# The order of the units in a projection of memory rows, their value stores, and the stack of their staging pools

## The chip, the cores and the metric

One core of one Trainium2 chip. The metric is the device time of one execution of the whole program in microseconds (us), the median of several runs. A profiled execution gives the trace; its times count from the first instruction of the span.

## The reference

Two independent parts are computed and joined along the last axis. Part A is a long convolution (H3), part B a transformer with a recurrent memory, in segments of 32 rows:

```python
def _A_ref(q, k, v, shift_k, ssm_k, ssm_D):          # 2048 x 1024
    ...                                              # k_shift: causal convolution of k with 4 taps
    kv = k_shift * v
    ...                                              # y: causal convolution of kv with ssm_k, by FFT of length 4096
    y = y + kv * ssm_D[None, None, :]
    return q * y

def _B_ref(x, mem0, Wq, Wk, Wv, Wo, seg_len):        # x 2048 x 1024, 32 heads of 128, 8 memory rows, seg_len 32
    ...
    mem = mem0
    for s in range(n_seg):                           # 64 segments
        xs = x[:, s * seg_len:(s + 1) * seg_len, :].copy()
        h = jnp.concatenate([mem, xs], axis=1)       # 40 rows
        q = jnp.einsum('btd,dhe->bhte', h, Wq)
        k = jnp.einsum('btd,dhe->bhte', h, Wk)
        v = jnp.einsum('btd,dhe->bhte', h, Wv)
        ...                                          # masked softmax attention within the 40 rows
        o = jnp.einsum('bhte,hed->btd', o, Wo)
        mem = o[:, :M, :].copy()
        outs.append(o[:, M:, :])
```

Each segment needs the memory rows that the segment before it gives, so the 64 segments run one after the other.

## The kernel before

The program has a prologue, which computes part A and prepares part B, and then the loop over the 64 segments. The order of the instructions on every engine is the order in which the program text issues them.

**What is prepared for part B.** Of a segment's 40 rows the first 32 (8 memory rows and 24 of x) are projected within the segment. The last 8 rows of all segments depend on x alone, so they are projected together in the prologue: hTB holds them transposed, 1024 by 512 (8 rows of each of 64 segments). This is the class `Rows` (L127). Its work is cut into 12 *units* (L85), one for each of queries (q), keys (k) and values (v) and each of four groups g of eight heads. A unit has eight steps j of eight matmuls of 128x512 each, and `half` (L155) does half a step, four matmuls; so there are 192 halves. The matmuls of the q and k units are on L177, those of the v units on L174. PSUM has two tiles for them. After every second half the sum is copied to a staging tile by `evac` (L148), on ACT (L150), or, in the last stage, on ACT and DVE by turns (L152).

The q unit and the k unit of a group write into the same staging tile stq (16 KB a partition), which is taken when a q unit begins (L168). When the k unit ends, one transfer on ACT's queue (L185) stores it to QKBd in DRAM, 2 MB in pieces of 256 bytes. A v unit writes the staging tile stv (8 KB a partition), taken when the unit begins (L170). When it ends, 16 transfers of 64 KB on POOL's queue (L190) store it to VBd. Both pools have one buffer each, so the next q unit's first copy waits for the last store from stq, and the next v unit's for the stores from stv. In the tail, the value staging also serves once as park_s (L671).

**Where the weights come from.** A unit needs eight pieces of 128x1024. `load_to` (L132) issues their loads on SP some pieces ahead. Pieces of *resident* weight pairs stay in SBUF for the whole program; pieces of *streamed* and *parked* pairs go into the small ring pring of eight buffers and are loaded again later. Resident pairs get their place in steps, as part A frees memory: `open_res` (L99) opens 9, 10, 3, 12, 2 and at the end the remaining 9 pairs, early ones first and then in the order in which the units use them (L94, L96). `relay` (L116) copies streamed pairs to a compact DRAM copy, from POOL's queue.

**The prologue's stages and the halves that each takes in between:**
- a0 (from L257): tables, and the first transform of ssm_k; no halves.
- a1 (L484 to L502): shift convolution and first transform of kv; 76 halves: q0, k0, v0, q1 and 12 of k1.
- c2 (L597 to L613): the frequency stage, one half in each of 36 steps: the rest of k1, v1, v2. In each step DVE forms products (L572), POOL or DVE adds them to Yre and Yim (L575, L576), and TensorE transforms back (L585).
- c3 (L617 to L648): the output stage, 8 halves ahead and 40 within 16 steps t: v3, q2, k2. A step loads zt and qt on SP (L629, L631), does halves, then the last transform (L644), a product on DVE (L647) and a store to the output on POOL (L648).
- the tail (L665 to L693): the last 32 halves, q3 and k3, and in between the parked weights, which are transposed (L687, L688, L691) and kept in PSUM.

Then all pools of the prologue are closed (L695), a ring of five 4 KB tiles (wring) is opened for the streamed weights and the last nine resident pairs are opened behind it (L696, L697). Before the first segment SP issues five loads into the ring (L713), the first read of QKBd (L793) and the 18 half loads of the nine Wo pairs (L113), in this order; POOL issues the first read of VBd (L803). Within the segments each ring tile that has been used is loaded anew (L713), so SP's queue carries the weight stream, 17 pairs of 512 KB a segment, of which two come from PSUM instead in turn with it.

**The stack of the staging pools.** SBUF pools grow from both ends. The pools of the projection lie at the right end; opened in the order hTB (8 KB), stq (16 KB), pring (16 KB), stv (8 KB), so stv lies lowest, next to the memory that the ring and the last nine pairs get from the left. The ring's 20 KB and the nine pairs' 36 KB cover 8 KB that c3 used and these 48 KB. With the order before, the ring covers stv and the lowest 4 KB of pring; the nine pairs cover the rest of pring, stq and hTB. The ring waits tile by tile for what it covers (`reuse_waits="tile"`), the pool of the nine pairs as a whole.

Of the kernel before, what the change touches and what calls it, by code (L numbers as in the profile page):

```python
# [21 lines left out]
def fused_kernel(ctx: ExitStack, tc, q, k, v, shift_k, ssm_k, ssm_D, outa, x, mem0, Wq, Wk, Wv, Wo, outb, n_seg):  # L22
# [11 lines left out]
    nc = tc.nc  # L34
# [18 lines left out]
    VBd = dram.tile([n_seg, 4, 4, 8, 256], BF, name="VBd")  # L53
# [9 lines left out]
    def half_src(key, n):  # L63
# [3 lines left out]
        if m == "v":  # L67
# [7 lines left out]
    mask = const.tile([128, 2, 40], BF, name="mask")  # L75
    make_identity(nc, ident[:])
    cp = ExitStack()
    hb = cp.enter_context(tc.tile_pool(name="b_hb", bufs=1, side="right"))
    hTB = hb.tile([128, 8, n_seg * 8], BF, name="hTB")
    stq = cp.enter_context(tc.tile_pool(name="b_stq", bufs=1, side="right"))  # L80
    pring = cp.enter_context(tc.tile_pool(name="b_pring", bufs=8, side="right"))
    stv = cp.enter_context(tc.tile_pool(name="b_stv", bufs=1, side="right"))
    ps_p = cp.enter_context(tc.tile_pool(name="b_ps_p", bufs=2, space=PSUM, side="right"))

    units = [("q", 0), ("k", 0), ("v", 0), ("q", 1), ("k", 1), ("v", 1), ("v", 2), ("v", 3),  # L85
             ("q", 2), ("k", 2), ("q", 3), ("k", 3)]

    def piece(i):
        (m, g), kc = units[i // 8], i % 8
# [37 lines left out]
    class Rows:  # L127
# [27 lines left out]
        def half(self, n, by="A"):  # L155

            for _ in range(n):
                if self.at == 192:
                    return
                iu, j, lo = self.at // 16, self.at % 16 // 2, self.at % 2 * 4  # L160
                m, g = units[iu]
                self.load_to(iu * 8 + 8)
                ws = self.loaded[iu * 8:iu * 8 + 8]
                assert len(ws) == 8
                if lo == 0:
                    self.ps = ps_p.tile([128, 512], F32, tag="pp", name="ps_" + m)
                if m == "q" and self.at % 16 == 0:
                    self.st = stq.tile([128, n_seg, 8, 2, 8], BF, tag="stq", name="stq")  # L168
                if m == "v" and self.at % 16 == 0:
                    self.sv = stv.tile([128, 4, 1024], BF, tag="stv", name="stv")  # L170
                rb, cs = j // 2, slice(j % 2 * 512, j % 2 * 512 + 512)
                for kc in range(lo, lo + 4):
                    if m == "v":
                        nc.tensor.matmul(self.ps[:], lhsT=hTB[:, kc, rb * 128:(rb + 1) * 128], rhs=ws[kc][:, cs],  # L174
                                         start=(kc == 0), stop=(kc == 7))
                    else:
                        nc.tensor.matmul(self.ps[:], lhsT=ws[kc][:, j * 128:(j + 1) * 128], rhs=hTB[:, kc, :],  # L177
                                         start=(kc == 0), stop=(kc == 7))
                if lo:
                    if m == "v":  # L180
                        self.evac(self.sv[:, rb, cs], self.ps[:], by)
                    else:
                        self.evac(self.st[:, :, j, int(m == "k"), :], self.ps[:].rearrange("e (s r) -> e s r", r=8), by)
                    if m == "k" and j == 7:
                        nc.scalar.dma_start(QKBd[:, :, g, :].rearrange("s e x -> e s x"),  # L185
                                            self.st[:].rearrange("e s h t r -> e s (h t r)"))
                    if m == "v" and j == 7:
                        for rb_ in range(4):
                            for c in range(4):
                                nc.gpsimd.dma_start(VBd[16 * rb_:16 * rb_ + 16, c, g],  # L190
                                                    self.sv[:, rb_, c * 256:(c + 1) * 256])
                self.at += 1
                self.load_to(self.at // 16 * 8 + 8 + self.at % 16 // 2 + 4)

# [62 lines left out]
    with ExitStack() as ck:  # L257
# [185 lines left out]
        for t in range(17):  # L443
# [16 lines left out]
            if t in (8, 10, 12, 14):  # L460
                rb = t // 2 - 4
# [535 lines left out]
@with_exitstack  # L997
def kernel(
    ctx: ExitStack,
    tc: tile.TileContext,  # L1000
    A_q: bass.AP,
    A_k: bass.AP,
    A_v: bass.AP,
    A_shift_k: bass.AP,
    A_ssm_k: bass.AP,
    A_ssm_D: bass.AP,
    B_x: bass.AP,
    B_mem0: bass.AP,
    B_Wq: bass.AP,
    B_Wk: bass.AP,  # L1010
    B_Wv: bass.AP,
    B_Wo: bass.AP,
    B_seg_len,
    out: bass.AP,
):
    assert int(B_seg_len) == 32
    S = B_x.shape[1]
    n_seg = S // 32
    outa = out[0, :, 0:1024]
    outb = out[0, :, 1024:2048]  # L1020
    with ExitStack() as fctx:
        fused_kernel(fctx, tc, A_q[0], A_k[0], A_v[0], A_shift_k, A_ssm_k, A_ssm_D, outa, B_x[0], B_mem0[0],
                     B_Wq.rearrange("d h e -> d (h e)"), B_Wk.rearrange("d h e -> d (h e)"),
                     B_Wv.rearrange("d h e -> d (h e)"), B_Wo.rearrange("h e d -> (h e) d"),
                     outb, n_seg)
# [35 lines left out]
```

## Time and profile before

| | us |
|---|---|
| median of 3 runs | 2194.64 |
| lowest and highest run | 2191.91, 2197.0 |
| the profiled execution | 2189.17 |
| its span, first to last instruction | 2187.2 |
| TensorE busy (matmuls) | 1783.4 (82% of the span) |
| VectorE busy | 1090.5 (50%) |
| ScalarE busy | 835.3 (38%) |
| GpSimd busy | 405.9 (19%) |
| moved by DMA | 732.15 MB, mean 335 GB/s |

The page's chain of waits has PE with 47% and DMA with 36% of the span; its dearest line is the stream of value weights into the ring (17%).

Names in the profile: PE is TensorE (PEld its weight loads), DVE VectorE, ACT ScalarE, POOL GpSimd, SP the engine that issues most loads; "q" behind a name is that engine's queue of transfers. `out<-in` names the tile written and the tile read, L with a number the line of the kernel; copies by `evac` all have its lines (L150, L152), so they are told apart by their tiles. The clock is the share of full speed that TensorE was granted. In a list of waits the three numbers are the total, the times and the longest, in us.

### The profile page before, as it was taken

How to read it: one execution, taken by the hardware profiler on the slowest of the kernel's cores; microseconds unless marked ns; L12 is line 12 of the kernel's file. 1: busy time of each engine (PE TensorE's matmuls, PEld its weight loads, DVE VectorE, ACT ScalarE, POOL GpSimd, SP SyncE). 2: the span in 40 equal slices, each digit the busy share in tenths (PEclk: the TensorE clock that was granted, in tenths of full speed). 3: DMA queues.
4: the chain of work that ended last, by engine and by line, in shares of the span. 5: the costliest groups of instructions: out<-in, count | busy, mean ns of one | idle time of the engine just before them, and what ended most of it. 6: DMA issues, size and time to landing. Idle time of an engine off the chain costs nothing.

```text
span 2187.2 us, 87959 instructions
## 1 busy us (share of the span) xinstructions
PE 1783.4 (82%) x37808; PEld 1048.2 (48%) x37808; DVE 1090.5 (50%) x3235; ACT 835.3 (38%) x2538; POOL 405.9 (19%) x841
## 2 busy tenths in 40 slices
PE   5777778758888888888888888888888888888889
PEld 2332223325555555554555555545555555555558
DVE  6885652224454555544455455444554545444540
ACT  5445551123333333333444333333333333334320
POOL 4013562101111111111111111111111111111110
PEclk8989899879999999999999999999999999999999
DMA  7798969889999999999999999999999999999990
GB/s 256 266 312 273 314 233 330 267 288 353 347 356 343 373 374 365 368 364 347 370 372 371 370 354 370 362 358 355 368 366 354 363 356 357 371 362 367 359 335 21
DMA packets 275653, 732.15 MB, mean 335 GB/s; under 512 B 65680, under 2 KB 85024, under 8 KB 275262
## 3 DMA queue, kind: packets, MB, share of 16 engines
q1 hardware_dynamic: 214414, 683.05, 84.7%
q0 software_dynamic: 18368, 28.88, 4.2%
q10 hardware_dynamic: 42480, 14.62, 2.7%
q8 instruction: 295, 4.83, 0.9%
q14 instruction: 96, 0.78, 0.1%
HBM read 676.14 MB, written 59.18 MB: 336 GB/s over the span
## 4 chain that ended last, share of the span: by engine, by line
PE 47%; DMA 36%; issue 6%; DVE 4%; ACT 4%; POOL 1%; SPq 0%; ACTq 0%; DVEq 0%; POOLq 0%
DMA wring<-Wstv 17%; PE qkacc L750 13%; PE yacc L867 9%; DMA wring<-Wstqk 7%; PE vacc L765 4%; PE otacc L850 3%; PE yacc L765 3%; PE tp L779 3%; PE pl L984 3%; DMA QKBd<-stq 2%; DMA H<-in_B_x_dram 2%; PE ps_k L177 2%; PE otacc L852 1%; DMA wring<-Wsto 1%; PE ps_q L177 1%
## 5 line engine op out<-in xcount | busy, mean ns | idle before, releaser
L750 PE MATMUL qkacc<-Wqk,hT 128*32 128x512 bf16 x4096 | 351.8, 384 | 3.6 <-issue 3.5
L855 ACT CAST OT<-otacc 128x80 bf16<-128x80 f32 x1024 | 183.8, 235 | 387.4 <-PE otacc L852 381.3
L858 POOL COPY OL<-OT 128x64 bf16<-128x64 bf16 x252 | 63.9, 253 | 1362.3 <-ACT OT L855 1362.3
L765 PEld LDWEIGHTS <-hT 128*32 128x32 bf16 x8192 | 213.8, 97 | 168.7 <-issue 101.9
L750 PEld LDWEIGHTS <-hT 128*32 128x32 bf16 x8192 | 178.3, 96 | 209.9 <-issue 66.7
L867 PE MATMUL yacc<-Wo,OT 128*32 128x256 bf16 x5632 | 253.3, 282 | 26.6 <-issue 21.2
L867 PEld LDWEIGHTS <-OT 128*32 128x32 bf16 x8192 | 213.1, 99 | 90.4 <-issue 58.4
L750 PE MATMUL qkacc<-wring,hT 128*32 128x512 bf16 x2048 | 207.1, 390 | 22.7 <-DMA wring<-Wstqk 20.3
L850 PE MATMUL otacc<-PT,vsb 32*128 32x64 bf16 x2048 | 147.7, 193 | 55.5 <-ACT OT L855 48.7
L765 PE MATMUL vacc<-wring,hT 128*32 128x256 bf16 x2560 | 118.0, 277 | 74.7 <-DMA wring<-Wstv 73.5
L788 DVE COPY QT<-tp 128x256 bf16<-128x256 bf16 x256 | 74.7, 292 | 204.7 <-PE tp L779 198.7
L719 ACT COPY wring<-park 128x1024 bf16<-128x1024 bf16 x128 | 129.9, 1015 | 116.2 <-PE qkacc L750 110.0
L750 PE MATMUL qkacc<-Wearly,hT 128*32 128x512 bf16 x2048 | 167.7, 403 | 7.7 <-DVE hT L893 3.4
L756 ACT CAST qks<-qkacc 128x512 bf16<-128x512 f32 x256 | 150.3, 587 | 47.6 <-PE qkacc L750 44.5
L823 DVE TENSOR_REDUCE mx<-S 128x4 f32<-128x160 f32 x256 | 83.1, 325 | 163.8 <-PE S L820 160.7
L765 PE MATMUL vacc<-Wv,hT 128*32 128x256 bf16 x3584 | 158.4, 274 | 0.7 <-issue 0.7
L834 DVE TENSOR_REDUCE sm<-P 128x4 f32<-128x256 bf16 x256 | 107.5, 420 | 100.6 <-ACT P L832 100.6
L852 PE MATMUL otacc<-PT,VB 32*128 32x64 bf16 x2048 | 144.2, 189 | 11.2 <-issue 10.5
L867 PE MATMUL yacc<-wring,OT 128*32 128x256 bf16 x2520 | 137.1, 281 | 16.4 <-issue 15.4
L885 DVE COPY hT<-x_tp 128x192 bf16<-128x192 bf16 (+1 forms) x64 | 23.0, 359 | 233.8 <-PE x_tp L884 233.8
L970 POOL DMA_DIRECT2D out_dram<-Y_sb x256 | 129.1, 511 | 39.6 <-ACT Y_sb L964 36.3
L850 PEld LDWEIGHTS <-vsb 32*128 32x128 bf16 x2048 | 84.3, 92 | 103.8 <-issue 94.1
(220 smaller groups left out, 2931.9 us busy)
## 6 DMA issues: line engine op xcount, KB each, us to landing
wring<-Wstqk SPq DMA_DIRECT2D x448, 512.0 KB, 6.4
wring<-Wstv SPq DMA_DIRECT2D x320, 512.0 KB, 6.0
wring<-Wsto SPq DMA_DIRECT2D x315, 512.0 KB, 6.0
SK<-s_sb SPq DMA_DIRECT2D x8, 1024.0 KB, 6.5
SU<-s_sb SPq DMA_DIRECT2D x8, 1024.0 KB, 7.8
QKBd<-stq ACTq DMA_DIRECT2D x4, 2048.0 KB, 16.3
Kg<-SK SPq DMA_DIRECT2D x16, 512.0 KB, 6.1
Ug<-SU SPq DMA_DIRECT2D x16, 512.0 KB, 7.2
```

What stands on the lines that cost most here:

```text
L719: nc.scalar.copy(t[:, 0, :], park[key][0][:])
L750: nc.tensor.matmul(u.qk[p0:p0 + 32, :], lhsT=hT[:, kc, :], rhs=w[t][:, c2 * 512:(c2 + 1) * 512], start=(kc == 0), stop=(kc == 7), tile_pos ...
L756: nc.scalar.copy(u.qks[:], u.qk[:])
L765: nc.tensor.matmul(u.vacc[32 * c:32 * c + 32, 0:256], lhsT=hT[:, kc, :], rhs=w[kc % 2][:, c * 256:(c + 1) * 256], start=(kc == 0 and Y is ...
L788: nc.vector.tensor_copy(u.QT[:].rearrange("e (c j) r -> e c j r", c=2), tv[:, 0])
L823: nc.vector.tensor_reduce(out=mx[:], in_=S[:], op=ALU.max, axis=AX.X)
L834: nc.vector.tensor_reduce(out=sm[:], in_=P[:], op=ALU.add, axis=AX.X)
L850: nc.tensor.matmul(o, lhsT=u.v[r, i * 128:(i + 1) * 128], rhs=PTv[r, i, 0], start=True, stop=False, tile_position=(32 * c, 0))
L852: nc.tensor.matmul(o, lhsT=VB[r, i * 128:(i + 1) * 128], rhs=PTv[r, i, 1], start=False, stop=True, tile_position=(32 * c, 0))
L855: nc.scalar.copy(u.OT[:, 2 * c:2 * c + 2, :], ov[:, :, 0:40])
L867: nc.tensor.matmul(Y[32 * dq:32 * dq + 32, 256:512], lhsT=u.OT[:, hh, 0:32], rhs=w[hh % 2][:, dq * 256:(dq + 1) * 256], start=(u.g == 0 an ...
L970: nc.gpsimd.dma_start(outb[32 * s:32 * s + 24, dq * 256:(dq + 1) * 256], Y_sb[32 * dq + 8:32 * dq + 32, :])
```

## The change

Three edits in the prologue. The units are taken group by group, q, k, v of group 0, then of group 1, and so on; before, v2 and v3 came right behind v1, and q2, k2, q3, k3 last. The 16 stores of a v unit, issued together behind its last copy, become four times four, each behind the copies of 128 rows. And the staging pools are opened as stq, stv, hTB, pring, so that pring lies lowest and stq at the very end.

```diff
     cp = ExitStack()
+    stq = cp.enter_context(tc.tile_pool(name="b_stq", bufs=1, side="right"))
+    stv = cp.enter_context(tc.tile_pool(name="b_stv", bufs=1, side="right"))
     hb = cp.enter_context(tc.tile_pool(name="b_hb", bufs=1, side="right"))
     hTB = hb.tile([128, 8, n_seg * 8], BF, name="hTB")
-    stq = cp.enter_context(tc.tile_pool(name="b_stq", bufs=1, side="right"))
     pring = cp.enter_context(tc.tile_pool(name="b_pring", bufs=8, side="right"))
-    stv = cp.enter_context(tc.tile_pool(name="b_stv", bufs=1, side="right"))
     ps_p = cp.enter_context(tc.tile_pool(name="b_ps_p", bufs=2, space=PSUM, side="right"))
 
-    units = [("q", 0), ("k", 0), ("v", 0), ("q", 1), ("k", 1), ("v", 1), ("v", 2), ("v", 3),
-             ("q", 2), ("k", 2), ("q", 3), ("k", 3)]
+    units = [(m, g) for g in range(4) for m in "qkv"]
...
-                    if m == "v" and j == 7:
-                        for rb_ in range(4):
-                            for c in range(4):
-                                nc.gpsimd.dma_start(VBd[16 * rb_:16 * rb_ + 16, c, g],
-                                                    self.sv[:, rb_, c * 256:(c + 1) * 256])
+                    if m == "v" and j % 2 == 1:
+                        for c in range(4):
+                            nc.gpsimd.dma_start(VBd[16 * rb:16 * rb + 16, c, g],
+                                                self.sv[:, rb, c * 256:(c + 1) * 256])
```

The order of the units also sets the order in which resident pairs are opened: the ten pairs that a1 opens, of which the last three were v2's, now end with three of group 2's query and key pairs, c2's three are the rest of those instead of v3's, and c3's twelve are v2's, group 3's query and key pairs and v3's.

## The prediction

> **What bounds the kernel now.** I read the page for its share of engines, then busy time by stage, then the chain of waits in the prologue, then who waits for whom. The page gives a span of 2187.2 us for the profiled execution, whose own time is 2189.17 us, so 2.0 us lie around the span; the median of the runs is 2194.64 us, 5.5 us above it. Sums are made on the profiled execution and carried over to the median as differences.
>
> By stage (from the span's start; columns as in the first line, then granted clock, share of the DMA engines, GB/s):
>
> ```profile
> core 0: us, PE busy (x) PEld busy (x) DVE busy (x) ACT busy (x) POOL busy (x), PEclk, DMA share, GB/s
> 185.00:313.00 128.00, 106.39 (x548) 32.59 (x549) 91.41 (x153) 82.04 (x152) 78.75 (x87) 0.92 0.83 273
> 313.00:393.00 80.00, 58.03 (x249) 24.64 (x247) 17.91 (x15) 13.87 (x24) 25.49 (x49) 0.91 0.95 333
> 393.00:441.00 48.00, 34.02 (x194) 17.04 (x192) 9.90 (x14) 4.76 (x9) 5.81 (x11) 0.86 0.69 222
> 441.00:471.00 30.00, 7.42 (x142) 3.94 (x146) 4.56 (x14) 5.01 (x8) 0.00 (x0) 0.63 0.93 281
> ...
> 545.00:1000.00 455.00, 387.49 (x9598) 236.04 (x9594) 227.87 (x773) 176.16 (x611) 71.22 (x173) 0.96 0.97 360
> ```
>
> The last row is the segment loop: its DMA engines are 97% busy, its TensorE 85%. What it has to move is fixed, so it ends as much earlier as it starts. The change lies in the rows above: the frequency stage c2 (185 to 313), the output stage c3 (313 to 393, DMA share 0.95), a tail of projection (393 to 441), and a start of the loop in which TensorE works 7.4 of 30 us.
>
> The chain of waits shows what holds these stages (start, length, what):
>
> ```profile
> 196.54 20.36 DMA QKBd<-stq
> ...
> 257.31 6.42 DMA VBd<-stv
> ...
> 316.65 6.05 DMA VBd<-stv
> ...
> 393.11 16.26 DMA QKBd<-stq
> ...
> 441.03 11.15 DMA QKBd<-stq
> ```
>
> These are stores of the two staging tiles, each held once, so the next unit of the same kind waits for them. Who waited (total, times, longest):
>
> ```profile
> ACT stv L150 <- DMA VBd<-stv: 19.6, 2, 12.4
> ...
> ACT stq L150 <- DMA QKBd<-stq: 16.4, 1, 16.4
> ...
> PE park_t L687 <- ACT stq L150: 13.2, 1, 13.2
> ...
> PE z_ps L585 <- POOL Yre L575: 8.8, 2, 7.9
> ```
>
> and the same for SP's queue:
>
> ```profile
> SPq L631 <- DVE ot L647: 28.4, 12, 9.5
> SPq L793 <- DMA QKBd<-stq: 24.2, 1, 24.2
> ...
> SPq L678 <- DMA QKBd<-stq: 12.6, 1, 12.6
> ```
>
> The first three are the staging tiles' reuse (v2 behind v1, v3 behind v2, q3 behind k2). L793 is the first read of QKBd in SP's queue: 18 Wo loads and the loop's weight stream stand behind it, and the first segment waits until 470.5 us for a stream tile.
>
> **The change, part by part.** Units keep their count and size: 192 half units of 0.863 us of TensorE, the same loads. The stages take them in fixed numbers, 76 before c2, 36 in c2, 48 in c3, 32 in the tail. So units 0 to 5 do not move; unit 6 (end of c2) turns from v2 into q2, unit 7 from v3 into k2, 8 and 9 from q2, k2 into v2, q3, and the tail from q3, k3 into k3, v3. Resident weight pairs are opened in fixed numbers too (10, 3, 12); the counts come out equal (three pairs of unit 6 or 7 in c2, twelve in c3), so no load is late that was not.
>
> *c2.* Unit 6 no longer writes the value tile, so the wait on v1's 16 stores goes. Its price: the output matmuls (L585) come every 3.07 us (249.10, 252.18, 255.25); behind the wait they come at 266.31, 271.46, 274.53 where 3.07 us steps give 264.46 for the last. **Gain 10.1 us**, 7.9 of idle and the rest at half clock. q2 writes the query tile, whose store landed at 216.9, 40 us earlier. The value stores of v1 now stand on POOL in fours between the products Yre and Yim: 4 x 0.53 = 2.1 us every four halves (12.3 us), where POOL is busy 3 x 1.15 of every 6.14 us and so idle 2.7. I cost them at nothing; were that cover gone, four groups x 2.1 = 8.4 us.
>
> *c3.* The start, where TensorE stood 10.1 us behind v2's stores, I count as nothing by itself: from 320 us the DMA share is 1.01 to 1.03, and the first SZ load took about 14 us, so it would have met the loads anyway. The stage is counted as DMA work.
> Removed: a hole at 356 to 368 us (shares 0.77, 0.36, 0.88: 4.0 us lost), which came as v3's 16 stores stood on POOL ahead of two output stores, DVE's product waited for those (9.8 us), and SP's L631 for DVE (9.5). Groups of four leave room: **4.0 us**. One MB of value stores fewer (before v2 and v3, after v2): at 333 GB/s **3.1 us**.
> Added: k2's query and key store, 2.1 MB, now in the middle (half 128, during t = 3) instead of at the end. Alone it runs at 220 GB/s (444 to 450 us, share 1.05); between 393 and 409.5 the queues moved 326 GB/s where 395 was usual. Below, it costs its bytes at 395, 5.3 us; above, its whole landing, 16.3. I take what that mixture lost, 16.4 x (395 - 326)/395 = 2.9, on top of the bytes, 8.2, say **8.5 us**. And SP stops during such a store: at all three that have something behind them (113, 196.5, 393 us) it issues four to seven more transfers and then stands 12.4, 10.4 and 12.6 us until the landing. What is queued there is zt and qt of later t and weights, and TensorE and DVE wait for these; the engines stay full on what was issued, and only restarting costs: at 216 to 220 the share was 0.46, **2.2 us** (0 to 5).
> Net +8.5 + 2.2 - 4.0 - 3.1 = **+3.6 us** (bounds -1.8 and +18.5). c3 ends at 393.3 - 10.1 + 3.6 = 386.8.
> The Trainium skill, "DMA: Bandwidth & Descriptors", section "Why small descriptors are slow (HBM only)", puts a fixed 3 cycles on a packet of 8 for 256 bytes. By that the store would take 5.3 x 11/8 = 7.3 us and the sum would gain 1.2 us; the 220 GB/s of this trace say more.
>
> *Tail.* Before: 393.3 to 441.0, 47.7 us. The tile wait goes, because k3 writes the tile that q3 already holds, and k2's store is long past: 13.2 us of TensorE idle, and 2.0 us because the 2.2 us of work behind it took 4.2 at a granted clock of 0.50. **15.2 us.** What is late next: the four parked weights. The first was issued 1.1 us after the stage began and landed some 6 us later; the four halves ahead of it take 3.45, so TensorE waits **3.6 us** (0 to 6) where the store had hidden it. The tail is then 47.7 - 15.2 + 3.6 = 36.1, and the projection ends at 422.9.
> The skill's "TensorE: Matmul & The Clock Gate", section "Part 1: The HAM clock gate (the "warmup" mystery)", lets about 3.4 us of idleness bring the half clock back; by that this new wait would cost some 2 us more. The trace grants 0.78 behind a pause of 4.9 us (369.5).
>
> *Behind the last row.* Before, SP's Wo loads began at 452.7, 11.7 after the projection's end, for k3's store. After, k3's store leaves 16 halves (13.8 us) before the end and needs 11.2 alone, so v3 hides it; were v3 not there it would cost the 11.2 again. Instead the nine late weight pairs lie on both staging tiles and hTB, and wait for v3's last row: 4 issues of 0.53 on POOL and a landing of 1.9 to 7.8, 4.0 to 9.9 in all; I take 7.0. **Gain 4.7.** With the restacked pools the ring's three covered tiles lie on the small weight ring pring alone, not on the value tile; the third of its five loads waits for v3's weights and so goes out at the projection's end and lands 3.4 to 6 us later, where its first use stands 2.7 us behind that end (443.7 for 441.0): up to 3 us that fall into the wait for the stream tile, so nothing.
> Value stores of v0 were already leaving pair by pair (from 118.6 on), since POOL had nothing else there: no price.
>
> **Sum**: 10.1 - 3.6 + 15.2 - 3.6 + 4.7 = **22.8 us** less. Profiled execution 2189.2 to 2166.4; for the median 2194.6 - 22.8 = **2172 us**.
>
> **The rivals.**
> *The store in c3 costs its whole landing* (15 in 100). For: c3 is DMA-bound, so nothing hides it; the one at 196.5 landed after 20.4 and stopped TensorE at 216. Against: the engines stayed full meanwhile. 16.3 for 8.5: 15.0 less, 2179.6. The skill's "DMA: Bandwidth & Descriptors", section "Issuing engines are not separate DMA queues", speaks for it: ACT's store runs on the engines that serve SP. The trace agrees (share 1.13 to 1.24 at 399 to 408).
> *Cheaper than bounded* (10): bytes only, no restart, parked weights in time: 3.2 + 2.2 + 3.6 more, 31.8 less, 2163.
> *c2's gain comes back in c3* because loads that the pause let through are then missing (6): DMA share was 0.83 there, which speaks against. 12.7 less, 2182.
> *POOL as the new stop* (6, slower). v2's four groups stand ahead of the output stores just while k2's store slows every landing; each opens a hole as v3's burst did, 9.5 us by L631. 4 x 9.5 = 38: 15 more than before, 2210. It decides from (22.8 + 4.4)/4 = 6.8 us a group on. For: the hole of before is of this kind. Against: it came with 16 stores in a row.
> *It does nothing* (3): the waits move and add up to the same, about 2194; against it stands that three separate waits go.
>
> **How the numbers follow.** My forecast has 60 in 100, its own range 2165 to 2179. With the cheaper case, and most of the first and third rival, 2161 to 2184 leaves out less than 2 in 10. A measurement of this kernel tells a difference from about 0.2%, 4.4 us. Faster by more: 60 + 15 + 10 + 6 = 0.91; within 0.03; slower 0.06.
>
> **What would show it.** Right: no wait of stv or stq on their stores at 257, 316 and 393; SP standing about 10 us in c3 during k2's store; no hole of 9.5 at L631; Wo loads beginning near 430 and the first segment's stall ending near 448. Wrong: c3 longer than 90 us, output stores waiting for value stores, or a segment loop whose pace is not the one before.

## The result, and the profile after

| | before | after |
|---|---|---|
| median of 4 runs each, us | 2193.27 | 2169.79 |
| lowest and highest | 2183.92, 2197.0 | 2166.93, 2172.11 |
| the profiled execution | 2189.17 | 2169.6 |
| its span | 2187.2 | 2167.7 |

The ratio is 0.9898, 95% interval 0.9868 to 0.9928. Of 2193.27 us that is 22.4 us less (the medians themselves differ by 23.5), where the forecast said 22.8.

Two profiles of equal code differ by some microseconds in a1 (the first inverse transform of c2 came between 188.6 and 195.7 us in all kernels here) and in the loop of 1700 us. So the stages are compared by marks of their own, in each kernel's trace: c2 from the first to the last inverse transform (`z_ps<-Yre`), c3 from there to the last `y_ps`, the tail from there to the first segment's `x_tp`, "behind" from `x_tp` to SP's first Wo load, and the way from `x_tp` to the end of the first segment's stall, which contains "behind". "All" runs from the first inverse transform to the end of that stall, and is the sum of the other columns without "behind".

| us | c2 | c3 | tail | behind | x_tp to stall's end | all |
|---|---|---|---|---|---|---|
| before | 117.0 | 83.2 | 48.1 | 11.6 | 29.4 | 277.7 |
| after | 105.7 | 88.3 | 38.7 | 8.1 | 24.5 | 257.2 |
| difference | -11.3 | +5.1 | -9.4 | -3.5 | -4.9 | -20.5 |
| forecast | -10.1 | +3.6 | -11.6 | -4.7 | -4.7 | -22.8 |

The stages give 20.5 us of the 22.4; the rest is well within the interval, which is 6.6 us wide to either side.

Busy time by stage of the changed kernel, to be laid beside that of before (c2, c3, tail, start of the loop, loop):

```profile
core 0: us, PE busy (x) PEld busy (x) DVE busy (x) ACT busy (x) POOL busy (x), PEclk, DMA share, GB/s
185.00:303.00 118.00, 105.69 (x564) 33.21 (x564) 91.82 (x153) 82.67 (x153) 79.75 (x89) 0.98 0.88 297
303.00:390.00 87.00, 58.52 (x243) 24.03 (x241) 20.29 (x17) 12.89 (x22) 17.40 (x32) 0.86 0.98 338
390.00:425.00 35.00, 32.27 (x227) 16.50 (x231) 8.73 (x13) 5.34 (x9) 11.82 (x23) 0.95 0.80 228
425.00:450.00 25.00, 7.20 (x132) 3.62 (x125) 3.87 (x14) 4.14 (x8) 1.37 (x3) 0.70 0.88 321
525.00:980.00 455.00, 384.01 (x9678) 235.65 (x9670) 230.91 (x782) 176.56 (x619) 71.22 (x172) 0.97 0.98 362
```

c2 does the same TensorE work in 118 instead of 128 us, at a clock of 0.98 instead of 0.92. The tail is 35 us with TensorE busy for 32. c3 alone grew. The loop's row is nearly that of before: 98% of the DMA engines and 362 GB/s, for 97% and 360.

The chain of waits between c2 and the loop (start, length, what):

```profile
193.14 19.81 DMA QKBd<-stq
...
384.52 5.93 DMA park_w<-in_B_Wv_dram
...
421.54 7.53 DMA wring<-Wstqk
...
435.21 5.26 DMA Wo<-in_B_Wo_dram
440.54 5.94 DMA wring<-Wstv
```

Of the five stores in the chain of before one is left, k1's. In place of k2's stands the landing of a parked weight, and in place of k3's the ring, Wo and stream loads. The waits from 180 to 460 us (total, times, longest) of the engines:

```profile
PE y_ps L642 <- DMA zt<-SZ: 25.2, 6, 12.1
...
PE park_t L685 <- DMA park_w<-in_B_Wv_dram: 3.4, 1, 3.4
...
PE z_ps L583 <- POOL Yre L573: 0.9, 1, 0.9
```

and of SP's queue:

```profile
SPq L627 <- DMA QKBd<-stq: 18.4, 1, 18.4
...
SPq L112 <- DMA VBd<-stv: 7.3, 1, 7.3
```

No copy waits for a store of its staging tile any more, and the 9.5 us at the qt load are gone. What is new is what SP stands behind k2's store in c3, 18.4 us where some 10 were foreseen; TensorE's longest wait for a zt (12.1) is its other end. And one line fell that the forecast had shown and used only for the size of its gain in c2: z_ps waiting for Yre, 8.8 us before, 0.9 after.

### The profile page after: what moved, and what is told of

The parts are those of the page before. It is cut to its first block, busy times and chain, and to the rows that moved or that the text cites. A ratio compares the mean times of both kernels' runs of the same rounds, so it can differ in the third digit from the quotient of the medians.

```text
span 2167.7 us, 87967 instructions
## 1 busy us (share of the span) xinstructions
PE 1781.4 (82%) x37808; PEld 1048.6 (48%) x37808; DVE 1091.4 (50%) x3235; ACT 835.5 (39%) x2538; POOL 407.9 (19%) x841
## 4 chain that ended last, share of the span: by engine, by line
PE 46%; DMA 35%; issue 8%; DVE 5%; ACT 4%; POOL 1%; SPq 0%; ACTq 0%; DVEq 0%; POOLq 0%
DMA wring<-Wstv 16%; PE qkacc L748 13%; DMA wring<-Wstqk 9%; PE yacc L865 9%; PE vacc L763 4%; PE otacc L848 3%; PE yacc L763 3%; PE pl L982 3%; PE tp L777 2%; DMA wring<-Wsto 2%; DMA H<-in_B_x_dram 2%; PE ps_v L173 1%; PE ps_k L176 1%; PE otacc L850 1%; PE ps_q L176 1%
## 5 line engine op out<-in xcount | busy, mean ns | idle before, releaser
L865 PE MATMUL yacc<-Wo,OT 128*32 128x256 bf16 x5632 | 258.5, 287 | 24.3 <-issue 20.1
L832 DVE TENSOR_REDUCE sm<-P 128x4 f32<-128x256 bf16 x256 | 107.6, 420 | 102.9 <-ACT P L830 102.9
## 6 DMA issues: line engine op xcount, KB each, us to landing
QKBd<-stq ACTq DMA_DIRECT2D x4, 2048.0 KB, 20.5
```

What stands on the lines that cost most here:

```text
L832: nc.vector.tensor_reduce(out=sm[:], in_=P[:], op=ALU.add, axis=AX.X)
L865: nc.tensor.matmul(Y[32 * dq:32 * dq + 32, 256:512], lhsT=u.OT[:, hh, 0:32], rhs=w[hh % 2][:, dq * 256:(dq + 1) * 256], start=(u.g == 0 an ...
```

## The experiments

Each kernel ran 4 to 10 times, beside the kernel before on the same chip. The before's medians in the three sessions were 2194.54, 2194.82 and 2196.76 us.

| us | c2 | c3 | tail | behind | x_tp to stall's end | all | ratio to before, interval |
|---|---|---|---|---|---|---|---|
| order_only | 116.5 | 87.7 | 41.0 | 8.4 | 27.5 | 272.7 | 0.9956 [0.9920, 0.9993] |
| rows_only | 108.0 | 75.9 | 47.6 | 11.6 | 28.6 | 260.1 | 0.9883 [0.9837, 0.9928] |
| stack_only | 116.8 | 83.3 | 48.5 | 14.5 | 31.5 | 280.1 | 0.9981 [0.9948, 1.0014] |
| old_stack | 106.3 | 88.2 | 38.7 | 8.6 | 27.6 | 260.8 | 0.9918 [0.9886, 0.9949] |
| double_store | 107.6 | 94.5 | 38.3 | 7.9 | 24.7 | 265.1 | 0.9955 [0.9931, 0.9980] |
| split_store | 108.7 | 90.3 | 37.1 | 7.9 | 25.0 | 261.1 | 0.9906 [0.9878, 0.9933] |
| park_later | 106.6 | 88.2 | 33.9 | 8.0 | 25.4 | 254.1 | 0.9889 [0.9834, 0.9945] |
| wo_by_tile | 107.2 | 87.2 | 38.6 | 0.5 | 21.6 | 254.6 | 0.9896 [0.9859, 0.9934] |
| after_again | 107.5 | 86.2 | 38.7 | 7.9 | 24.6 | 257.0 | 0.9895 [0.9849, 0.9942] |
| rows_again | 108.5 | 75.0 | 48.0 | 11.6 | 28.7 | 260.3 | 0.9896 [0.9845, 0.9948] |
| both | 107.7 | 86.5 | 34.0 | 0.5 | 20.9 | 249.1 | 0.9831 [0.9789, 0.9873] |
| best | 107.7 | 86.9 | 30.7 | 3.3 | 22.4 | 247.7 | 0.9847 [0.9796, 0.9899] |

**The order of the units alone.** The kernel before with the new `units`; stores and stack as they were.

```diff
-    units = [("q", 0), ("k", 0), ("v", 0), ("q", 1), ("k", 1), ("v", 1), ("v", 2), ("v", 3),
-             ("q", 2), ("k", 2), ("q", 3), ("k", 3)]
+    units = [(m, g) for g in range(4) for m in "qkv"]
```

> The new order of the units alone; the 16 value stores of a unit stay together behind its last copy, and the stack is the old one. Theory A (what stops c2 is POOL: v1's 16 stores stand in front of the product Yre, whatever unit comes next): the pause of about 8 us at 257 us in c2 stays, with TensorE waiting for POOL's Yre, no longer for the value tile; c2's gain is at most 2 us, and v2's 16 stores open a hole of about 9 us behind them in c3. Only the tail's gain (13 of idle, 2 of half clock, less some 5 for the parked weights) and some 3 us behind the last row remain: 5 to 11 us less than before, 2182 to 2188. Theory B (the prediction: it is the reuse of the value tile that stops c2): the pause goes with the order, c2 gains 10 us, and the sum is 15 to 20 us less, 2173 to 2178.

c2 stays at 116.5 us, although the unit behind v1 is now q2 and writes another tile. POOL's timeline shows what the pause hangs on (start, length, line, what, how many; in brackets the idle time before and who ended it):

```profile
250.59 1.15 POOL L574 TENSOR_TENSOR Yre<-pa,pb 128x512 bf16<-128x512 bf16 x1 [0.70 <-DVE pb L571]
251.69 5.23 POOL L189 DMA_DIRECT2D VBd<-stv  x10
257.19 0.53 POOL L189 DMA_DIRECT2D VBd<-stv  x1 [0.27 <-ACT Kim L560]
260.27 2.76 POOL L189 DMA_DIRECT2D VBd<-stv  x5 [2.55 <-DMA VBd<-stv]
263.19 1.07 POOL L121 DMA_DIRECT2D Wstv<-in_B_Wv_dram  x2 [0.16 <-issue]
264.27 1.16 POOL L574 TENSOR_TENSOR Yre<-pa,pb 128x512 bf16<-128x512 bf16 x1
```

Sixteen stores stand in POOL's order ahead of the next Yre. Their issues alone are 8.5 us, the last five of them wait 2.55 us until an earlier store has landed, and the issues of two weight copies behind them take 1.1, so Yre comes 13.7 us after the one before it, where a step takes 3.07. In the kernel before POOL's order is the same, with 13.5 us from one Yre (251.62) to the next:

```profile
252.72 4.20 POOL L190 DMA_DIRECT2D VBd<-stv  x8
...
260.96 2.60 POOL L190 DMA_DIRECT2D VBd<-stv  x5 [2.09 <-DMA VBd<-stv]
...
265.10 1.16 POOL L575 TENSOR_TENSOR Yre<-pa,pb 128x512 bf16<-128x512 bf16 x1
```

TensorE's side of it, in the list of waits of order_only:

```profile
PE z_ps L584 <- POOL Yre L574: 9.0, 2, 8.1
```

There is no wait of a copy for its staging tile in this kernel's list, and the pause is whole. Beyond c2 the tail lost 7.1 us and "behind" 3.2, and c3 grew by 4.5. The hole that was expected in c3 came as well: behind v2's sixteen stores (370.4 to 381.5 us) an output product waited 11.1 us for the output stores, SP stood 8.4 us at a qt load, and the share of the DMA engines fell to 0.44 from 388 to 392 us.

**The stores by rows alone.** Order and stack as before, the stores in fours. It was run in two sessions (rows_only, rows_again), the second time beside the changed kernel (after_again).

```diff
-                    if m == "v" and j == 7:
-                        for rb_ in range(4):
-                            for c in range(4):
-                                nc.gpsimd.dma_start(VBd[16 * rb_:16 * rb_ + 16, c, g], ...)
+                    if m == "v" and j % 2 == 1:
+                        for c in range(4):
+                            nc.gpsimd.dma_start(VBd[16 * rb:16 * rb + 16, c, g], ...)
```

> The value stores by 128 rows alone, with the old order and the old stack. Theory A (POOL's burst stops c2): with four groups of four the pause at 257 us shrinks to 2 us or less, c2 gains 8 or more; at the start of c3 v3's first copy still waits some 6 us for v2's last row, and the hole of 9.5 us at SP's qt loads goes. The tail stays as before, with 13 us behind k2's store: 10 to 14 us less than before, 2179 to 2183. Theory B (reuse of the value tile): v2's first copy comes 6 us behind v1's last one and still waits most of a store's landing, 5 to 7 us; c2 gains 3 us at most: 4 to 8 us less.

> The grouping of the value stores alone, with the order and the stack of before, timed on the same chip as the changed kernel. Theory (the burst of sixteen stores on POOL is what held c2 and c3): ratio 0.988 to 0.992, c2 106 to 109 us, c3 75 to 78 us, tail 47 to 49 us. Rival (its earlier time was luck of the run): ratio above 0.994.

> The changed kernel itself, timed beside the others. If the order of the units and the stack add something to the grouping of the stores, its ratio lies below that of the grouping alone by about 0.001 (3 us of 2190, from 257.2 against 260.1 us up to the end of the stall); if they add nothing, the two are equal within their intervals of some 0.003. Ratio 0.988 to 0.991.

Here v2 still follows v1 on the one tile, and c2 is nevertheless 108.0 us (108.5 the second time). POOL's timeline:

```profile
242.32 1.16 POOL L574 TENSOR_TENSOR Yre<-pa,pb 128x512 bf16<-128x512 bf16 x1 [0.70 <-DVE pb L571]
243.41 2.12 POOL L189 DMA_DIRECT2D VBd<-stv  x4
245.54 1.16 POOL L574 TENSOR_TENSOR Yre<-pa,pb 128x512 bf16<-128x512 bf16 x1
```

Four stores fit between two Yre at a step of 3.2 us. The tile's wait is short as well, since only the last four of the stores are still out when v2's first copy comes; the waits that remain in this kernel are those of k2's store in the tail:

```profile
ACT stq L150 <- DMA QKBd<-stq: 15.5, 1, 15.5
...
PE park_t L686 <- ACT stq L150: 12.4, 1, 12.4
...
ACT stv L150 <- DMA VBd<-stv: 3.2, 2, 2.8
```

This part brings 17.6 us of the 20.5 up to the stall's end, more than the 10 to 14 that were expected. Timed side by side, the grouping alone (median 2175.42) and the whole change (2175.37) can't be told apart: the intervals reach some 10 us to either side, so they could not have shown the 3 us by which the traces differ (260.1 and 260.3 against 257.2 and 257.0).

**The stack.** old_stack is the changed kernel with the pools opened as before; stack_only is the kernel before with the new stack.

```diff
-    stq = cp.enter_context(tc.tile_pool(name="b_stq", bufs=1, side="right"))
-    stv = cp.enter_context(tc.tile_pool(name="b_stv", bufs=1, side="right"))
     hb = cp.enter_context(tc.tile_pool(name="b_hb", bufs=1, side="right"))
     hTB = hb.tile([128, 8, n_seg * 8], BF, name="hTB")
+    stq = cp.enter_context(tc.tile_pool(name="b_stq", bufs=1, side="right"))
     pring = cp.enter_context(tc.tile_pool(name="b_pring", bufs=8, side="right"))
+    stv = cp.enter_context(tc.tile_pool(name="b_stv", bufs=1, side="right"))
```

> The change without the restacked pools: new order, stores by 128 rows, old stack. The third and fourth ring tile then lie on the value tile and wait for v3's last stores, where they waited for v3's weights: SP's queue stands some 7 us longer in front of them, and the Wo loads begin 1 to 2 us later than in the changed kernel, since three ring loads and the first QKBd read then go out behind the same wait. Theory: 1 to 3 us slower than the changed kernel, about 2171 to 2173, all of it behind the projection's end. Rival (the stack carries a good part of the gain): 8 us or more slower, 2178 or above. Second rival (the stack is worth nothing): no difference.

> The restacked pools alone, with the old order and stores. In the old order the last unit is k3: the ring's third tile then lies on k3's weights and is loaded some 14 us later, still ahead of the QKBd read that SP waits for, so nothing changes before 452 us, and the first value tiles of the stream land after the first segment wants them, within the stall that is there anyway. Theory: within 3 us of before, 2190 to 2197. Rival (the stack itself is worth several us): 5 us or more less.

With the new order the old stack costs 3.1 us, all of it behind the projection's end (27.6 against 24.5): the stream tiles then lie on the value tile, and SP's ring loads stand 21.9 us for `VBd<-stv` by its list of waits. With the old order the new stack gains nothing (280.1 against 277.7, "behind" longer by 2.9; the timed interval includes no change; why it is longer was not followed up). So the new order and the new stack belong together: old_stack's 260.8 us is no better than the grouping's 260.1 without either, as what the order takes off the tail (47.6 to 38.7) it puts on c3 (75.9 to 88.2).

**The store in c3, twice.** The changed kernel stores group 2's staging tile a second time, to a table nobody reads.

```diff
+                        if g == 2:
+                            nc.scalar.dma_start(QKBx[:].rearrange("s e x -> e s x"),
+                                                self.st[:].rearrange("e s h t r -> e s (h t r)"))
```

> The changed kernel, with the store of k2's staging tile issued a second time into a DRAM tile that nobody reads; the result is the reference's. It prices one 2 MB store of 256-byte pieces within c3. Theory (c3 is bound by its DMA work, so the store costs what it takes from the engines, 8 to 12 us, wherever it is hidden from ACT): c3, from the last inverse transform of c2 to the last transform of c3, grows from 88.3 to 96 to 102 us, and the longest stop of SP in c3 from 18.4 to 26 us or more. Rival (what costs is only SP's stop and its restart, not the bytes): 2 to 4 us more. Second rival (hidden anyway): 0 to 1.

c3 becomes 94.5 us, 6.2 more than in the changed kernel's first profile (88.3) and 8.3 more than in its second (86.2): less than I expected. SP had not one stop of 26 us but two, of 12.0 and 10.0. The stage's windows show where a store's price lies (c3 as in the table; rows_only first, the changed kernel second, this kernel third; the last three columns are TensorE's clock, the share of the DMA engines and GB/s):

```profile
303.00:378.90 75.90, 59.48 (x258) 25.24 (x258) 17.48 (x15) 14.82 (x26) 22.46 (x41) 0.93 0.97 344
```

```profile
295.00:383.30 88.30, 61.88 (x258) 25.54 (x258) 18.37 (x15) 15.17 (x26) 20.81 (x38) 0.86 0.95 320
```

```profile
300.80:395.30 94.50, 63.67 (x258) 26.32 (x258) 18.37 (x15) 14.99 (x26) 20.52 (x37) 0.82 0.99 318
```

The engines are nearly full in all three (shares 0.95 to 0.99). What changes is the bytes (75.9 x 344 = 26.1 MB, 28.3, 30.1) and the rate, 344 against 320 GB/s. From the first to the second, 2.15 MB more at 344 GB/s are 6.2 us, and 28.3 MB at 320 instead of 344 take 6.2 us more; together the 12.4 by which the stage is longer. That the rate falls because the store moves pieces of 256 bytes is likely (alone, such a store ran at 220 GB/s in the kernel before) but not shown by itself, as these two kernels differ in the order too. The third differs from the second by the store alone. Length times share gives the time for which the engines were busy: 83.9 us in the second, 93.6 in the third. So a store takes about 9.7 us of them, near the 9.5 that 2.1 MB take at 220 GB/s, and the stage grew by less because the second kernel's engines had 4.4 us to spare.

**The store in pieces.** If SP's stop were what costs, smaller stores, each landing sooner, should let SP go on.

```diff
-                        nc.scalar.dma_start(QKBd[:, :, g, :].rearrange("s e x -> e s x"), ...)
+                        for s0 in range(0, n_seg, n_seg // 4 if g < 3 else n_seg):
+                            ss = slice(s0, s0 + (n_seg // 4 if g < 3 else n_seg))
+                            nc.scalar.dma_start(QKBd[ss, :, g, :].rearrange("s e x -> e s x"), ...)
```

> The changed kernel, with the query and key stores of groups 0 to 2 issued as four transfers of 512 KB each, by 16 segments, instead of one of 2 MB. Theory (SP and ACT have eight transfers in flight between them, taken in turn, so a transfer of SP waits for the one eight places ahead to land): SP waits for a quarter's landing, its longest stop in c3 falls from 18.4 to 8 us or less, the hole in the DMA at 344 to 352 us closes, c3 falls from 88.3 to about 85, c2 from 105.7 to about 102 since its own stop behind k1's store (10 us) shrinks too. Rival (SP is held by the engines' backlog, not by the count): the stops keep their lengths, 16 us or more in c3, and no stage moves by more than 1 us.

SP's waits for QKBd are gone, but c3 is 90.3 us and c2 108.7, where 85 and 102 were expected: in c3 the stop went to ACT. Its queue stood 18.5 us over the issue of the four pieces (one store takes 0.37),

```profile
327.24 18.48 ACTq L186 DMA_DIRECT2D QKBd<-stq  x4
```

and the copies of v2 came behind it in ACT's order, for which TensorE's matmuls waited:

```profile
PE ps_v L173 <- ACT stv L149: 14.9, 1, 14.9
```

So this run exchanges one stop for another. It doesn't tell what SP's alone costs, nor does any run show that the limit is eight transfers.

**The parked weights later.** The changed kernel with eight halves instead of four ahead of the parked weights.

```diff
-    rows.half(4, "AD")
+    rows.half(8, "AD")
     for i, (key, n) in enumerate(halves):
```

> The changed kernel, with 8 instead of 4 halves ahead of the first parked weight in the tail; no work is added or left out. Theory: the pause of 3.4 us goes, and the half clock behind it (0.68 and 0.50 at 390 to 394 us), which costs another 2 us: the tail, from the last transform of c3 to the first segment, falls from 38.7 to about 33.5. Rival (the clock would have fallen anyway, from waits in c3): only the 3.4 us, about 35.3. Second rival (the parked weights are just asked for later and the wait moves to the third or fourth): 1 us or less.

The tail falls from 38.7 to 33.9 us. The windows of the changed kernel around its wait, and last one of the altered kernel in the same work:

```profile
386.00:390.00 4.00, 1.08 (x6) 0.29 (x3) 0.69 (x1) 0.00 (x0) 0.51 (x1) 1.00 1.04 393
390.00:394.00 4.00, 3.50 (x15) 1.71 (x16) 0.69 (x1) 0.00 (x0) 1.69 (x4) 0.59 0.47 160
```

```profile
389.00:393.00 4.00, 4.00 (x20) 1.79 (x19) 1.66 (x2) 0.99 (x2) 0.54 (x1) 1.00 1.05 396
```

After the pause the clock is 0.59; in the altered kernel TensorE's list has no wait of park_t for a load, and its windows from 385 to 405 us all show 1.00. So the wait's price is 4.8 us: 3.4 of idle, and the other 1.4 fit the lower clock. The Trainium skill's "TensorE: Matmul & The Clock Gate", section "Part 1: The HAM clock gate (the "warmup" mystery)", lets the half clock come back after an idle window of about 3.4 us; the trace agrees, with 0.59 behind a wait of 3.4 us. The prediction's estimate of what that costs was some 2 us, and 1.4 were found.

**The last nine pairs tile by tile.** In the changed kernel the pool of the nine Wo pairs waits as a whole for what it covers. Here it waits tile by tile, and the two pairs that lie on the value tile are loaded last.

```diff
-            pool = cw_.enter_context(tc.tile_pool(name=f"b_wres{len(to_open)}", bufs=1))
+            pool = cw_.enter_context(tc.tile_pool(name=f"b_wres{len(to_open)}", bufs=1, reuse_waits=waits))
...
-    open_res(len(to_open))
+    open_res(len(to_open), "tile")
...
+    for i in (0, 1, 2, 5, 6, 7, 8, 3, 4):
+        for n in range(2):
+            res_half(last_o[i], n)
```

> The changed kernel, with the last nine weight pairs waiting each for what its own place covered, not for the whole pool, and the two pairs that lie on the value tile loaded last. Theory: the first Wo load goes out about 1 us behind the first QKBd read instead of 8, and the first segment's stall ends 3 to 7 us earlier as counted from the projection's end (24.5 us in the changed kernel); less than 8, since the DMA engines were idle for only some 4 us of these. Rival (the wait for the value stores only hid what the engines are short of): the stall ends within 1 us of where it did.

SP's timeline, first of the changed kernel, then of this one:

```profile
422.09 0.41 SPq L791 DMA_DIRECT2D qkb<-QKBd  x1
430.10 10.03 SPq L112 DMA_DIRECT2D Wo<-in_B_Wo_dram  x18
440.54 0.33 SPq L711 DMA_DIRECT2D wring<-Wstv  x1
```

```profile
427.67 0.41 SPq L791 DMA_DIRECT2D qkb<-QKBd  x1
428.12 14.66 SPq L112 DMA_DIRECT2D Wo<-in_B_Wo_dram  x18
443.19 0.33 SPq L711 DMA_DIRECT2D wring<-Wstv  x1
```

Wo begins 7.6 us sooner behind the read of QKBd, but the eighteen issues take 14.7 instead of 10.0 us, so the next stream load is sooner by 2.9 us only (15.5 against 18.5 after that read), and that is what the stall's end gains (21.6 against 24.5), a little under the 3 to 7 that were expected.

**Both, and one more.** "both" joins the last two alterations. "best" also moves four halves from the tail to the start of c3, where TensorE stands 8.2 us for the first zt.

```diff
-        rows.go(4)
+        rows.go(6)
         for t in range(16):
...
         nc.vector.tensor_copy(park_s[:, i, :], tw[:])
-        rows.half(2, "AD")
+        rows.half(1, "AD")
```

> The changed kernel with two alterations: eight halves instead of four ahead of the parked weights, and the last nine pairs opened tile by tile with their loads in another order. Theory (the tail's wait for the parked weights and the Wo loads' wait for the last value store lie one behind the other, so removing both adds up): tail 33 to 35 us (38.7 in the changed kernel), first Wo load under 1 us behind the projection's end (8.1), from the first inverse transform to the end of the first segment's stall 249 to 253 us (257.2), ratio 0.986 to 0.989 where the changed kernel gives 0.989 to 0.991. Rival (the loop takes up what the prologue gives, since its stream of weights sets its pace): the prologue shorter by as much and the ratio that of the changed kernel.

> As the kernel with the two alterations, and four halves moved from the tail into the start of the output stage c3, where TensorE stands some 8 us for the first zt. Theory (c3 is bound by its transfers, so TensorE's work there is free): c3 as in the changed kernel, 87 to 90 us, tail 30 to 31.5 us, from the first inverse transform to the end of the stall 245 to 250 us, ratio 0.984 to 0.988. Rival (the four halves' weights, some 0.5 MB, come out of c3's full transfers): c3 longer by 1.5 to 3.5 us, nothing left of the gain.

The two gains at least add up. Tail and stall together take 63.2 us in the changed kernel, 59.3 with the one, 60.2 with the other and 54.9 with both: 8.3 us less, where the two alone give 6.9. The median is 2162.26 us, 0.9831 of before, against 2175.37 and 0.9895 of the changed kernel in the same session; the slowest run of "both" (2167.55) lies below the fastest of the changed kernel (2168.88). That is more than the 0.986 to 0.989 forecast, and more than the 8 us of the traces. The four halves are free in c3 (86.9 against 86.5) and shorten the tail by 3.3 us, but "behind" is 3.3 instead of 0.5. In part that is the read of QKBd, which stands ahead of Wo on SP and now waits 1.5 us for k3's store, by SP's list of waits, probably as the projection that hid it ends sooner. 1.4 us are left, and the timed runs (0.9847) can't tell it from "both".

## Why the prediction came out right, and where it did not hold

- **c2, -10.1 forecast, -11.3 and -9.5 in two profiles: right in size, wrong in cause.** The step that failed is "Unit 6 no longer writes the value tile, so the wait on v1's 16 stores goes", priced as the gain of 10.1. That wait did go in order_only and the pause stayed; the pause went in rows_only, where the value tile is still reused. What held the stage was the burst of sixteen store issues ahead of Yre on POOL: the fours take 9.0 us off c2 under the old order (117.0 to 108.0) and 10.2 under the new one (order_only's 116.5 to old_stack's 106.3), the order 0.5 and 1.7. Whether the wait for the tile would hold c2 once the burst is gone was not tested, as the fours shorten both. The forecast costed the fours at nothing, which is what they cost, but did not see that their being fours was the gain. In the trace of before both stand in the same 30 us: a wait of ACT's copy for the tile, 7.2 us, and a wait of z_ps for Yre, 7.9 us. I took the first for the cause and the second for its consequence; the 7.9 was among the lines shown.
- **c3, +3.6 forecast, +5.1 and +3.0.** The size is near, but the parts do not stand as they were taken. The grouping was to give the hole's 4.0 us, and the order the 3.1 of the value stores; under the old order, where v2 and v3 keep their places, the grouping alone gives 7.3 and 8.2. Under the new order it gives nothing: order_only, with the burst and its hole, has 87.7 us, no more than the changed kernel. There SP's stop behind k2's store is 13.2 us instead of 18.4. In the changed kernel v2's fours are issued during that stop (329.9 to 344.3 us), in order_only the stores come after it; whether the fours make it longer was not tested. Order and stack were to add the store and SP's restart less the value stores, 8.5 + 2.2 - 3.1 = 7.6; from the grouping alone to the whole change c3 grows by 12.4 and 11.2. The store's term was too small (about 9.7 us of the engines for 8.5). And the upper bound of +18.5 leaves out the two gains; with them it is +11.4.
- **SP's stop was to be about 10 us and is 18.4.** What it costs by itself isn't settled: the pieces moved the stop to ACT, and the doubled store lengthened c3 by 6.2 to 8.3. It can be seen in the windows that the DMA engines were partly idle at its end, as the forecast's restart term said:

```profile
344.00:348.00 4.00, 0.00 (x0) 0.00 (x0) 0.00 (x0) 0.00 (x0) 0.34 (x1) 0.50 0.67 178
348.00:352.00 4.00, 0.00 (x0) 0.00 (x0) 0.00 (x0) 0.00 (x0) 0.00 (x0) 0.50 0.55 164
```

  At shares of 0.67 and 0.55 these 8 us of the changed kernel lose 0.33 x 4 + 0.45 x 4 = 3.1 us of transfers, where 2.2 were taken.
- **The tail, -11.6 forecast, -9.4.** The waits behind the store, put at 15.2 us, are gone. The parked weights' wait was 3.4 us, where 3.6 were taken; what was left out of the sum is the half clock behind it, 1.4 us by park_later. The forecast had read 0.78 behind the pause at 369.5 us, but that is a window from 368 to 372, of which the pause takes 1.5 us; from 370 to 374 the same trace grants 0.57. One us remains unaccounted for: 48.1 - 15.2 would be 32.9, and park_later has 33.9.
- **Behind the last row, -4.7 forecast, -3.5 to the Wo loads.** They wait for v3's last stores, 7.3 us in SP's list. At the stall's end the gain is 4.9, of which 3.1 come from the stack, which the forecast had costed at nothing for the ring's loads.
- **The rivals.** The store at its whole landing would have made c3 11.4 us longer (3.6 + 7.8); it was 5.1 and 3.0. The cheaper case (2163) and no change at all (2194) fall by the time, 2169.79. c2's gain did not come back in c3: rows_only has c2 and c3 both shorter. POOL did not become the new stop, as the fours cost nothing, but POOL was the old one in c2.
- **The sum** is right because the three edits come to the forecast together, and that is in good part luck. The forecast's terms give the grouping 4.0 us (the hole) and the order and the stack the other 18.8. Measured up to the stall's end, the grouping gives 17.6 us, the order on top of it nothing (260.8 against 260.1) and the stack 3.6 more (257.2).

## What to carry to other kernels

When two waits end at the same place, the trace shows both, and only taking one away alone tells which one holds the stage. Look at what stands ahead of the waiting work on every engine, cheap issues of transfers included. A burst of stores on an engine that also computes is better spread over the steps, in handfuls that fit into its idle time. When a change has several parts, price each part alone: a sum can come out right though its parts do not. And moving a transfer out of one stage's path puts its bytes and its stop into another; the change pays what that stage has to spare, here little, since c3's DMA engines were full.

## What the runs showed of the hardware that was not expected

- A store of 2 MB in 256-byte pieces on ACT's queue stops SP too: after four to seven further transfers SP stood until it had landed (18.4 us in c3 and 9.6 in c2 of the changed kernel, 12.6 in the tail of the kernel before). Cut in four, the stop was ACT's own, 18.5 us over four issues. What limit is at work was not settled.
- Sixteen small stores in a row on POOL do not only cost their issues (0.53 us each): in order_only the queue waited 2.55 us for a landing behind the eleventh, and from one Yre to the next it was 13.7 us.
- A wait of 3.4 us of TensorE cost 4.8 us, as the clock was 0.59 over the 4 us behind it (park_later against the changed kernel).
